# Attention loops issued in an order worked out from durations, with exponentials over three and two PSUM banks by turns, in place of fixed two-head steps

## Chip, cores, metric

One NeuronCore of a Trainium2 chip. The time is device microseconds (us) of one execution. The engines are PE (TensorE), ACT (ScalarE), DVE (VectorE), POOL (GpSimd) and SP (SyncE, which issues most DMAs). "PEld" is PE's weight load. The granted clock (PEclk) is the share of full speed that the profile shows PE was given.

## What is computed

Four layers in a row on x of 2048 x 512 (bf16), each `x = x + f(layernorm(x))`: spectral filter A, attention B, A, B again with the same weights.

```python
def _A_ref(x, w_r, w_i):                        # S = 2048, D = 512
    X = rfft2(x.astype(float32), axes=(-2, -1))
    return irfft2(X * (w_r + 1j * w_i), s=(S, D), axes=(-2, -1)).astype(bfloat16)

def _B_ref(x, wq, wk, wv, wo):                  # H = 32 heads of Dh = 16; k and v shared by all heads
    q = (x @ wq).reshape(B, S, H, Dh).transpose(0, 2, 1, 3)
    k, v = x @ wk, x @ wv
    p = softmax(einsum("bhqd,bkd->bhqk", q, k) * Dh ** -0.5, axis=-1)
    o = einsum("bhqk,bkd->bhqd", p, v)
    return o.transpose(0, 2, 1, 3).reshape(B, S, H * Dh) @ wo
```

## The kernel before

The Fourier transforms are matrix products. Attention is a loop over 32 series in each of the two B layers: a series is 512 queries x 4 heads. A *unit* is one block of 128 keys of one series and head: 128 x 512 scores, in one PSUM bank. There are 2048 units in a loop. A unit's exponentials are made in one of two ways:

- an *A unit* by ACT, with its exponential function, two units (two banks) in one instruction; one value product follows;
- a *D unit* by DVE, which turns scores into the bit pattern of a power of two (an int16 read as bf16). Four such tables, shifted against each other by 32 of 128 steps of an octave, are averaged through four value products. DVE makes the first table from PSUM; shifts of it come from DVE (128 x 2048 at a time) and POOL (128 x 1024).

Score products have 16 live of 32 contracted rows, so four fit beside each other into PE's rows; value products have 32 output columns, so four fit into PE's columns. I call four value products side by side a *quad*. A *turn* is a change of PE between products of different shape: score products, value products (and zero products like them, below), and products of the whole array such as projections.

The step of the loop is fixed by a plan: two A units of one ACT instruction, in most steps one D unit, and six value products. Twice in a usual series (`flags` false) there is no D unit; there a piece of a query or output projection is put in.

```python
    def plan(qb, s):                                     # key blocks for D units; which steps take one
        if (qb, s) == (NQB - 1, 7):
            return (1, 4, 7, 10), [a < 16 for a in range(24)]
        if (qb > 0 and s in (1, 2)) or (qb, s) == (0, 0):
            return (2, 5, 9, 12), [a % 3 != 2 for a in range(24)]
        return (1, 4, 7, 10, 13), [a % 11 != 10 for a in range(22)]

    def do_step(self, a_units, u, n):                    # [...] cut
        if u is not None:
            sd = self.ps.tile("b", [P, 512], F32)        # bank of the D unit
            self.scores(u, sd)
        if a_units:
            sa = self.ps.tile("sa", [P, 2, 512], F32)    # two banks, two buffers
            for m, au in enumerate(a_units):
                self.scores(au, sa[:, m, :])
            e = self.sb.tile("e", [P, 2, 512], BF)
            nc.scalar.activation(out=e, in_=sa, func=ACT.Exp, bias=EXP_LN, scale=SCALE)
        # [...] DVE's first table, shifts on DVE and POOL
        for z in pvs:                                    # of two steps ago, and D terms
            self.pv(*z)
        if u is None and self.first_pieces and self.step > 4:
            self.first_pieces.pop(0)()                   # transposes, keys, values of the last tokens
        elif u is None and self.pieces and self.step - self.last_piece > 4:
            self.last_piece = self.step
            self.pieces.pop(0)()                         # a whole projection: 4 or 5 products

    def qproj(self, qb, g, use_scalar):
        pq = self.ps.tile("b", [P, 512], F32)
        for cc in range(NC):                             # NC = 4
            nc.tensor.matmul(pq, lhsT=c.wq[:, cc, g * P:(g + 1) * P], rhs=xTq[:, cc, cols], ...)
```

PSUM's eight banks: scores "two" 2 x 2 banks, "one" 2 (accumulators of the loop; transposes of the spectral stage), "b" 2 (D scores, projections). The two spectral stages that matter here are `stage1` (transposes and a first product, one for each quarter `t` of the tokens) and `stage2`. All four query projections of the first queries stand ahead of the loop.

The softmax here doesn't subtract the row's maximum and nothing guards it: scores larger than these inputs give would overflow.

## Time and profile before

Median of five runs 1621.35 us (1615.95 to 1624.67). In the profile, 1620.2 us:

| stretch | us | ACT busy | PE busy |
|---|---|---|---|
| first loop, first exponential to end of the last | 679.2 | 98% | 99% |
| from there to the second loop | 113.5 | 34% | 86% |
| second loop | 680.7 | 98% | 99% |

The table of busy times by stretch, kernel before (start:end, length, then busy us and instructions of each engine, granted PE clock, DMA share, GB/s):

```profile
core 0: us, PE busy (x) PEld busy (x) DVE busy (x) ACT busy (x) POOL busy (x), PEclk, DMA share, GB/s
...
124.40:803.60 679.20, 672.16 (x6051) 192.34 (x6048) 631.18 (x1077) 666.08 (x723) 325.20 (x315) 0.99 0.05 16
803.60:917.10 113.50, 97.23 (x613) 51.51 (x612) 80.67 (x172) 38.47 (x53) 8.21 (x17) 0.95 0.01 3
917.10:1597.80 680.70, 671.48 (x6049) 191.93 (x6046) 618.27 (x1039) 666.33 (x723) 324.78 (x315) 0.99 0.06 18
```

PE and ACT are both full in the loops, so busy time does not say which of them sets the pace. The chain of waits (the work that ended last, followed back), by engine, names PE:

```profile
PE 79%; DVE 13%; DMA 3%; issue 3%; POOL 1%; ACT 1%; SPq 0%; DVEq 0%; POOLq 0%; ACTq 0%
```

The groups of the loop (busy us, mean ns of one | idle before, and what ended it):

```profile
L541 ACT ACTIVATE e<-sa 128x1024 bf16<-128x1024 f32 x1440 | 1329.4, 1142 | 24.2 <-PE sa L434 22.8
L516 POOL TENSOR_SCALAR t<-t 128x1024 int16<-128x1024 int16 x608 | 636.8, 1048 | 691.9 <-DVE t L511 513.8
L544 DVE TENSOR_SCALAR t<-b 128x512 int16<-128x512 f32 x1216 | 790.9, 681 | 61.6 <-PE b L434 56.1
...
L434 PE MATMUL sa<-QT,KT 32*128 32x512 bf16 x2880 | 563.7, 383 | 2.1 <-ACT e L541 2.1
```

ACT's exponential shows 1142 ns as a mean, but that is from start to end of instructions that overlap: 1440 of them are busy for 1329 us, 0.923 each. The timeline of ACT shows the rhythm (start, length of a run of instructions without idle time, count, idle time before it):

```profile
299.73 24.93 ACT L541 ACTIVATE e<-sa 128x1024 bf16<-128x1024 f32 x27
325.01 5.61 ACT L541 ACTIVATE e<-sa 128x1024 bf16<-128x1024 f32 x6 [0.36 <-PE sa L434]
330.98 5.61 ACT L541 ACTIVATE e<-sa 128x1024 bf16<-128x1024 f32 x6 [0.36 <-PE sa L434]
```

Read one instruction at a time, the ends of two exponentials lie 0.917 us apart wherever they follow without idle time. I call what a step takes beyond that a *gap*, and measure it from end to end. The gaps add up to 18.9 us in the first loop and 20.4 in the second (the prediction has 19.1 and 20.6; how small a gap is still counted makes the difference). About 6.4 us of each are in the first 25 us. Most others are 0.46 us, and the timeline of PE shows what stands there (here the gap at 324.7):

```profile
322.88 0.39 PE L434 MATMUL sa<-QT,KT 32*128 32x512 bf16 x2
323.20 0.39 PE L447 MATMUL acc<-e,V 128*32 128x512 bf16 x2
323.52 1.04 PE L494 MATMUL b<-wo_sb,ON 128*128 128x512 bf16 x4
324.49 0.39 PE L434 MATMUL b<-QT,KT 32*128 32x512 bf16 x1
324.49 0.39 PE L434 MATMUL sa<-QT,KT 32*128 32x512 bf16 x2
```

The next scores follow the last ones after 1.61 us, as a whole output projection (four products, 0.97 us to the next scores) lies between them.

### The profile page before, as it was taken

What the parts mean: (1) busy time and instruction counts of PE and PEld (TensorE: products, weight loads), DVE (VectorE), ACT (ScalarE), POOL (GpSimd) and SP (SyncE); (2) the same over time, 40 slices, a digit from 0 to 9 for tenths busy, and PEclk for the clock granted to TensorE, in tenths of its full rate; (3) what the DMA queues carried; (4) which work ended last, traced back from release to release, by engine and by line L of the source; (5) the groups of instructions that cost most, each with busy time, mean ns of one, the idle gap of its engine ahead of it and who ended that gap; (6) DMA issues with size and microseconds to landing.
All of it is one profiled execution on the core that took longest, in us unless ns stands there. A gap on an engine that the chain in (4) does not pass through costs nothing.

```text
span 1620.2 us, 34219 instructions
## 1 busy us (share of the span) xinstructions
PE 1541.9 (95%) x13320; PEld 488.3 (30%) x13320; DVE 1421.4 (88%) x2476; ACT 1425.7 (88%) x1570; POOL 682.3 (42%) x696
## 2 busy tenths in 40 slices
PE   4899999999999999999988999999999999999996
PEld 2542222222222222222344322222222222222221
DVE  6777999989998999899958789998899889998994
ACT  6248999999999999999823699999999999999994
POOL 3013545445553455445400145454445444544542
PEclk9998999999999999999999899999999999999998
DMA  6000000000000000000000000000000000000000
GB/s 190 0 1 1 17 16 17 17 16 17 17 17 10 17 17 17 17 17 17 17 7 1 1 8 17 17 17 27 19 13 18 21 23 16 17 20 25 18 16 29
DMA packets 44916, 31.75 MB, mean 20 GB/s; under 512 B 25553, under 2 KB 35793, under 8 KB 44625
## 3 DMA queue, kind: packets, MB, share of 16 engines
q1 hardware_dynamic: 44368, 28.51, 5.9%
q8 instruction: 104, 1.70, 0.4%
q0 software_dynamic: 384, 1.05, 0.2%
q14 instruction: 60, 0.48, 0.1%
HBM read 24.43 MB, written 2.62 MB: 17 GB/s over the span
## 4 chain that ended last, share of the span: by engine, by line
PE 79%; DVE 13%; DMA 3%; issue 3%; POOL 1%; ACT 1%; SPq 0%; DVEq 0%; POOLq 0%; ACTq 0%
PE acc L447 37%; PE b L434 21%; PE sa L434 9%; DVE t L544 4%; DVE t L511 3%; PE b L391 2%; PE one L328 2%; DMA rb<-rd 2%; PE two L266 2%; PE b L494 2%; PE two L242 1%; DVE odd L479 1%; DVE ON L476 1%; PE two L270 1%; PE two L268 1%
## 5 line engine op out<-in xcount | busy, mean ns | idle before, releaser
L541 ACT ACTIVATE e<-sa 128x1024 bf16<-128x1024 f32 x1440 | 1329.4, 1142 | 24.2 <-PE sa L434 22.8
L516 POOL TENSOR_SCALAR t<-t 128x1024 int16<-128x1024 int16 x608 | 636.8, 1048 | 691.9 <-DVE t L511 513.8
L544 DVE TENSOR_SCALAR t<-b 128x512 int16<-128x512 f32 x1216 | 790.9, 681 | 61.6 <-PE b L434 56.1
L447 PE MATMUL acc<-t,V 128*32 128x512 bf16 x4864 | 732.8, 385 | 0.0
L447 PE MATMUL acc<-e,V 128*32 128x512 bf16 x2880 | 569.2, 392 | 0.0
L434 PE MATMUL sa<-QT,KT 32*128 32x512 bf16 x2880 | 563.7, 383 | 2.1 <-ACT e L541 2.1
L434 PE MATMUL b<-QT,KT 32*128 32x512 bf16 x1216 | 467.3, 385 | 14.0 <-DVE t L544 11.9
L511 DVE TENSOR_SCALAR t<-t 128x2048 int16<-128x2048 int16 x608 | 417.3, 687 | 0.0
L434 PEld LDWEIGHTS <-KT 32*128 32x128 bf16 x4096 | 204.8, 90 | 619.9 <-issue 612.9
L447 PEld LDWEIGHTS <-V 128*32 128x32 bf16 x7744 | 159.8, 93 | 330.2 <-issue 330.2
L176 POOL TENSOR_TENSOR rstd<-mv,eps 128x4 f32<-128x4 f32 x16 | 3.3, 209 | 186.0 <-DVE mv L169 186.0
L168 DVE BATCH_NORM_STATS2 stats<-x_sb 128x6 f32<-128x512 bf16 x64 | 43.4, 687 | 15.5 <-ACT x_sb L330 8.5
L273 ACT CAST Xs<-two 128x1024 bf16<-128x1024 f32 x16 | 16.2, 1012 | 40.7 <-PE two L270 40.7
L266 PE MATMUL two<-Y,TAB 128*128 128x512 bf16 x128 | 48.5, 379 | 0.1
L456 DVE COPY den<-acc 128x512 f32<-128x512 f32 x64 | 43.6, 682 | 1.0 <-PE acc L447 1.0
L495 DVE TENSOR_TENSOR x_sb<-b,x_sb 128x512 bf16<-128x512 f32 x32 | 21.9, 690 | 23.5 <-PE b L494 23.3
L315 PE MATMUL two<-TAB,V 128*128 128x512 bf16 x128 | 33.8, 396 | 7.8 <-DVE V L288 7.8
L330 ACT CAST x_sb<-one 128x512 bf16<-128x512 f32 x32 | 18.5, 586 | 21.4 <-PE one L328 21.1
L242 PE MATMUL two<-tab_PH,xTA 128*128 128x512 bf16 x128 | 33.2, 414 | 4.0 <-DVE xTA L236 3.0
L270 PE MATMUL two<-Y,TAB 128*128 128x256 bf16 x128 | 34.9, 273 | 0.0
L268 PE MATMUL two<-Y,TAB 128*128 128x256 bf16 x128 | 34.9, 272 | 0.0
L494 PE MATMUL b<-wo_sb,ON 128*128 128x512 bf16 x120 | 33.4, 394 | 0.4 <-DVE x_sb L495 0.4
(82 smaller groups left out, 609.0 us busy)
## 6 DMA issues: line engine op xcount, KB each, us to landing
rb<-rd SPq DMA_DIRECT2D x64, 256.0 KB
x_sb<-in_A_x_dram SPq DMA_DIRECT2D x4, 512.0 KB
ON<-odd SPq DMA_DIRECT2D x120, 16.0 KB
TAB<-const_TAB SPq DMA_DIRECT2D x1, 1024.0 KB
wr_sb<-in_A_w_r_dram SPq DMA_DIRECT2D x4, 256.0 KB
wi_sb<-in_A_w_i_dram SPq DMA_DIRECT2D x4, 256.0 KB
dq<-den SPq DMA_DIRECT2D x64, 8.0 KB
rd<-dq SPq DMA_DIRECT2D x64, 8.0 KB
```

Source lines behind the costliest of these rows:

```text
L242: nc.tensor.matmul(pm[:, q, :], lhsT=xT[:, pair, q, cc, :], rhs=c.PH[:, cc, :], start=(cc == 0), stop=(cc == NC - 1))
L266: nc.tensor.matmul(pm, lhsT=TAB[:, t, j2, (COS + n) % 4, :], rhs=yt, start=(t == 0), stop=False, skip_group_check=True)
L268: nc.tensor.matmul(pm[:, LO], lhsT=TAB[:, t, j2, (SIN + n + 2) % 4, :], rhs=yt[:, HI], start=False, stop=False, skip_group_check=True)
L270: nc.tensor.matmul(pm[:, HI], lhsT=TAB[:, t, j2, (SIN + n) % 4, :], rhs=yt[:, LO], start=False, stop=(t == T - 1), skip_group_check=True)
L434: self.nc.tensor.matmul(out, lhsT=self.c.KT[32 * i:32 * i + 32, half, kc * P:(kc + 1) * P], rhs=self.A.QT[32 * i:32 * i + 32, g, qb * 512: ...
L447: self.nc.tensor.matmul(self.acc[key][32 * i:32 * i + 32, :], lhsT=self.c.V4[:, kc, j, :], rhs=e, start=first, stop=False, skip_group_chec ...
L456: nc.vector.tensor_copy(out=den, in_=self.acc.pop(key))
L494: nc.tensor.matmul(po, lhsT=o[:, r * P:(r + 1) * P], rhs=w, start=(k == 0), stop=(k == len(parts) - 1))
L511: nc.vector.tensor_scalar(out=tj, in0=cyc["t0"], scalar1=float(SH[j]), scalar2=None, op0=ALU.add)
L516: nc.gpsimd.tensor_scalar(out=cyc["t1"][:, h, :], in0=tj[:, h, :], scalar1=1.0, scalar2=float(SH[1] - SH[j]), op0=ALU.mult, op1=ALU.add)
L541: nc.scalar.activation(out=e, in_=sa, func=ACT.Exp, bias=EXP_LN, scale=SCALE)
L544: nc.vector.tensor_scalar(out=self.dcyc[c]["t0"][:, k, :], in0=sd, scalar1=Y_MUL, scalar2=Y_ADD, op0=ALU.mult, op1=ALU.add)
```

## The change

Intent: let ACT pay its fixed part less often (three banks, then two, in one instruction), pack value products into full quads, and issue on all engines in an order that a small model of their durations finds, so that none waits. The core of the diff (the model, some 500 lines, is cut; the lines shown are a selection, some shortened, with comments added):

```diff
     ps = Arena(ctx.enter_context(tc.tile_pool(name="ps", bufs=1, space=bass.MemoryType.PSUM)),
-               {"two": 2, "one": 2, "b": 2}, {"acc": "one", "sa": "two"})
+               {"a3": 1, "a2": 1, "acc": 1, "b": 2}, {})
@@ stage1 of the spectral filter
-            pt = ps_.tile("one", [P, 2, NC, P], BF)
+            pt = ps_.tile("b", [P, 2, NC, P], BF)
@@ ahead of the loop
-                for g in range(4):
-                    at.qproj(0, g, g % 2 == 0)
+                at.qproj(0, 0, nc.scalar.copy)
@@ after the first loop: the filter's memory is lent to the loop and loaded again
+            load_filter(nc.gpsimd, c, sb, A_w_r, A_w_i)
@@ the loop
+QUAD, ACT_FIX, ACT_UNIT = 0.225, 0.05, 0.4267
+PSUM_OP, WIDE_OP, POOL_OP = 0.6, 0.6, 1.05
+    def scores(self, with_a):                      # three A units, then two, and up to two D units
+            n, units, self.a_next = self.a_size, self.a_next, []
+            self.a_size = 5 - n
+            sa = self.ps.tile(f"a{n}", [P, n, 512], F32)
+    def quad(self, t, full):                       # one value product for each of the four heads
+    def filler(self):                              # zero weights: adds nothing to the accumulator
+        for i in range(4):
+            self.nc.tensor.matmul(out[32 * i:32 * i + 32, :], lhsT=self.c.zw, rhs=self.c.wo[:, 0, :], ...)
+    def pool(self):                                # POOL's shift waits for DVE's wide shift two back
+            if h >= 2:
+                ready = max(ready, self.halves[h - 2].get("s_end", NEVER) + 0.16)
+    def ask_queries(self):                         # a projection is two tasks of two products
+            m1 = self.add("PE", 2 * QUAD, first, at=at, bank=True)
+            m2 = self.add("PE", 2 * QUAD, lambda ...: self.A.qproj_mm(qb, g, tile["pq"], (2, 3)), [m1])
+    def run(self):                                 # the engine whose model time is least goes next
+        while self.v_cur < self.n_series:
+            turns[min(self.t, key=self.t.get)]()
```

In numbers of instructions: 582 exponentials of 1536 elements and 583 of 1024 in place of 1440 of 1024; 2912 A units and 1184 D units in place of 2880 and 1216; products with zero weights, which I call fillers.

## The prediction

> **What bounds the kernel now.** The two attention loops take 679 and 681 us of 1620 (124.4-803.6 and 917.1-1597.8 in the table of busy times by stretch). There ACT is busy 98%, PE 99%, DVE 91-93%, POOL 48%. The chain of waits gives PE 79%, but where a loop runs smoothly the 128x1024 exponentials end exactly 0.917 us apart (675 of 719 steps of the first loop in the timeline), each starting before the last has ended: ACT sets the pace, 1440 x 0.917 = 1320 us. The rest, 19.1 and 20.6 us, is where two ends lie further apart: 6.4 us at each loop's start (last tokens' transposes, keys, values), and twenty steps of 1.38 us where a projection sits on PE between score groups.
>
> **What the change does.** It replaces fixed steps (2 heads for ACT, mostly 1 for DVE, 6 value products) by an order worked out from durations.
>
> - ACT: exponentials of 1536 and 1024 alternate, 582 + 583 for 1440. Casts of 512 and 1024 take 0.586 and 1.012 us, so 512 elements cost 0.427; the fixed part of a pipelined exponential is 0.917-0.853 = 0.064. A 1536 then takes 1.343; the sum is 1316 us, only 4 less, as ACT now takes 2912 units, not 2880 (DVE 1184, not 1216).
> - PE: value products go in fours into the four column groups, in longer batches: 1290 turns between score and value products a loop, not 1440. The Trainium skill, "TensorEngine Tiling", section "Tiling Modes", says a mode switch drains TensorE; the trace agrees in size: two value products take 0.32 us in the chain, six 0.54, so a turn costs about 0.1. I count 951 value slots, 583 score slots, 250 filler slots, 150 projections of 0.215 us and the turns: 550 us of 660. PE gets slack despite 1940 fillers.
> - DVE: operations issue every 0.60 us; 592 conversions, 296 shifts and 80 us more: 610 us a loop, 92%, as before.
> - PSUM: scores hold 3 + 2 banks, one buffer each; the accumulator falls to one, so a series' end holds value products up for one evacuation (0.68 us).
> - Three first query projections move into each loop: 12 products of 0.22 us, 2.6 us each time.
> - Filters are loaded again through POOL; landed before use.
>
> **Critical path.** The gain is mostly the 40 us of ACT gaps, not the wider exponential. I expect about 15 us to return as small stalls: single score buffers leave PE 0.917 us to refill the wide one.
>
> 1621 - 4 (ACT work) - 40 (gaps) + 15 (new stalls) - 5 (projections) = 1587 us; range 1571 to 1612. Faster by over 2%: 0.53; within 2%: 0.43; slower: 0.04.
>
> **What would show it.** Loops of 664-670 us; ACT 98-99% busy there; narrow exponentials ending 0.92 us after a wide one, wide ones 1.34; no 6 us at the loop's start; stretches outside the loops a few us shorter, their groups unchanged.
>
> **What would make it wrong.** PE, in its fixed order, waits for DVE's bank or the single accumulator and ACT starves: idle above 30 us a loop. DVE and POOL collide: the skill's "SBUF — State Buffer", section "Who interferes with whom", says DVE's fast modes and GpSimd lock each other out (no run shows it yet). Shifts longer than 0.69 or 1.05 us would show it. A granted clock below 0.99 in the loops. A longer tail after the last exponential.

## The result

Median 1593.40 us (1591.18 to 1597.06, 8 runs) against 1622.04 (15 runs). The ratio is 0.9831, 95% interval 0.9816 to 0.9845. Ratios are the mean time of one kernel's fast runs over that of the other's of the same rounds, so not quite the ratio of the medians quoted. That is faster, by less than 2%.

The same stretches of the changed kernel, first loop, between the loops, second loop:

```profile
120.70:790.30 669.60, 640.36 (x7031) 197.54 (x7027) 624.94 (x1051) 663.26 (x586) 332.39 (x313) 0.99 0.07 19
790.30:908.50 118.20, 96.80 (x615) 51.01 (x605) 79.80 (x167) 38.08 (x52) 8.61 (x17) 0.94 0.01 3
908.50:1571.00 662.50, 632.68 (x6970) 196.88 (x6967) 616.94 (x1023) 658.77 (x583) 326.23 (x309) 0.99 0.06 19
```

The loops are 9.6 and 18.2 us shorter, ACT is busy over 99% in them, PE 96%; the stretch between the loops is 4.7 us *longer*. The chain of waits, by engine and by line, has turned over:

```profile
ACT 51%; PE 24%; issue 12%; DVE 8%; DMA 4%; POOL 1%; SPq 0%; POOLq 0%; DVEq 0%; ACTq 0%
ACT e L827 50%; PE acc L673 7%; PE a L614 5%; DMA rb<-rd 2%; PE a L282 2%; PE b L614 2%; PE acc L798 1%; DVE tB L851 1%; DVE spare L875 1%; PE acc L348 1%; DMA rd<-dq 1%; PE a L258 1%; DVE stats L177 1%; PE a L284 1%; PE a L286 1%
```

Half the span is now a chain of exponentials alone, where before the pieces of PE's steps made it up. The groups, with the two shapes of the exponential apart, and the fillers:

```profile
L827 ACT ACTIVATE e<-a 128x1536 bf16<-128x1536 f32 x582 | 967.6, 1663 | 9.1 <-PE a L614 4.5 <-PE b L614 4.4
L827 ACT ACTIVATE e<-a 128x1024 bf16<-128x1024 f32 x583 | 723.2, 1241 | 1.5 <-PE acc L673 1.2
...
L614 PE MATMUL a<-QT,KT 32*128 32x512 bf16 x2912 | 460.6, 383 | 48.5 <-ACT e L827 35.9 <-ACT x_sb L350 1.3
...
L899 POOL TENSOR_SCALAR tA<-tA 128x1024 int16<-128x1024 int16 x298 | 320.5, 1078 | 341.4 <-DVE tB L851 263.8 <-PE b L614 38.3 <-PE acc L673 26.3
...
L798 PE MATMUL acc<-wo_sb,zw 128*32 128x512 bf16 x1868 | 184.0, 388 | 0.0
```

The timeline of ACT in the first loop (a run is named after its first shape; wide and narrow alternate):

```profile
199.22 38.85 ACT L827 ACTIVATE e<-a 128x1536 bf16<-128x1536 f32 x34
238.52 67.90 ACT L827 ACTIVATE e<-a 128x1536 bf16<-128x1536 f32 x60 [0.46 <-PE a L614]
306.75 11.40 ACT L827 ACTIVATE e<-a 128x1536 bf16<-128x1536 f32 x10 [0.32 <-PE b L614]
```

The window cuts the first run: it began at 138.5 us and has 88 exponentials. Runs of 88 and 60 without a break, and later one of 294, have taken the place of runs of 6 to 121, mostly with 0.36 us between them. Ends lie 1.343 us apart at a wide one and 0.917 at a narrow one, so the exponentials alone are 582 x 1.343 + 583 x 0.917 = 1316 us, 4 less than 1440 x 0.917 = 1320. The gaps are 9.6 and 6.1 us, 15.6 in place of 39.2 (sums of unrounded values).

Where the 28.5 us between the two profiles come from:

| stretch | before, us | after, us | difference |
|---|---|---|---|
| start to first product of stage 2 | 43.3 | 42.9 | -0.4 |
| stage 2 to first exponential, first loop | 81.1 | 77.8 | -3.3 |
| first loop | 679.2 | 669.6 | -9.6 |
| last exponential to stage 2 | 33.5 | 40.0 | +6.5 |
| stage 2 to first exponential, second loop | 80.0 | 78.2 | -1.8 |
| second loop | 680.7 | 662.5 | -18.2 |
| last exponential to the end | 22.4 | 20.7 | -1.7 |

The one loss is behind the first loop. PE's timeline there, kernel before (803.65 is the end of the last exponential):

```profile
803.86 0.39 PE L447 MATMUL acc<-e,V 128*32 128x512 bf16 x2
...
804.84 0.61 PE L232 MATMUL one<-tab_ident,ec 128*128 128x128 bf16 x8
...
806.75 3.63 PE L242 MATMUL two<-tab_PH,xTA 128*128 128x512 bf16 x16 [0.60 <-DVE xTA L236]
...
815.34 0.60 PE L494 MATMUL b<-woz_sb,odd 128*128 128x512 bf16 x2 [1.82 <-DVE odd L479]
```

The last queries' output projection needs `odd`, and for `odd` the softmax's divisors go through DRAM and back, which takes some 10 us. Before, PE does the next layer's transposes (L232) in that time. The changed kernel:

```profile
790.39 0.39 PE L673 MATMUL acc<-e,V 128*32 128x512 bf16 x2
...
792.45 0.38 PE L344 MATMUL acc<-x_sb,tab_ident 128*128 128x512 bf16 x1
800.92 1.03 PE L740 MATMUL b<-woz_sb,odd 128*128 128x512 bf16 x2 [8.09 <-DVE odd L704]
...
805.97 0.61 PE L248 MATMUL b<-tab_ident,ec 128*128 128x128 bf16 x8
```

PE stands still for 8.1 us and begins the transposes (L248) at 806.0, 15.6 us after its last value product. Two half-done projections hold both "b" banks, and the transposes now need one of those.

### The profile page after: what moved, and what is told of

The parts are those of the page before. It is cut to its first block, busy times and chain, and to the rows that moved or that the text cites. A ratio compares the mean times of both kernels' runs of the same rounds, so it can differ in the third digit from the quotient of the medians.

```text
span 1591.7 us, 36765 instructions
## 1 busy us (share of the span) xinstructions
PE 1468.0 (92%) x15204; PEld 497.1 (31%) x15204; DVE 1412.5 (89%) x2430; ACT 1414.4 (89%) x1293; POOL 691.0 (43%) x689
## 3 DMA queue, kind: packets, MB, share of 16 engines
q0 software_dynamic: 1024, 3.15, 0.7%
## 4 chain that ended last, share of the span: by engine, by line
ACT 51%; PE 24%; issue 12%; DVE 8%; DMA 4%; POOL 1%; SPq 0%; POOLq 0%; DVEq 0%; ACTq 0%
ACT e L827 50%; PE acc L673 7%; PE a L614 5%; DMA rb<-rd 2%; PE a L282 2%; PE b L614 2%; PE acc L798 1%; DVE tB L851 1%; DVE spare L875 1%; PE acc L348 1%; DMA rd<-dq 1%; PE a L258 1%; DVE stats L177 1%; PE a L284 1%; PE a L286 1%
## 5 line engine op out<-in xcount | busy, mean ns | idle before, releaser
L827 ACT ACTIVATE e<-a 128x1536 bf16<-128x1536 f32 (+1 forms) x1165 | 1319.1, 1452 | 10.6 <-PE a L614 4.5
L614 PE MATMUL a<-QT,KT 32*128 32x512 bf16 x2912 | 460.6, 383 | 48.5 <-ACT e L827 35.9
L899 POOL TENSOR_SCALAR tA<-tA 128x1024 int16<-128x1024 int16 x298 | 320.5, 1078 | 341.4 <-DVE tB L851 263.8
L899 POOL TENSOR_SCALAR spare<-spare 128x1024 int16<-128x1024 int16 x294 | 318.1, 1085 | 317.6 <-DVE tB L851 253.5
L673 PE MATMUL acc<-tB,V 128*32 128x512 bf16 x2368 | 428.5, 386 | 0.1
L875 DVE TENSOR_SCALAR spare<-b 128x512 int16<-128x512 f32 x588 | 387.4, 684 | 32.5 <-PE b L614 28.9
L875 DVE TENSOR_SCALAR tA<-b 128x512 int16<-128x512 f32 x596 | 391.8, 682 | 26.6 <-PE b L614 21.7
L673 PE MATMUL acc<-tA,V 128*32 128x512 bf16 x1192 | 257.5, 389 | 1.6 <-DVE den L691 1.4
L673 PE MATMUL acc<-spare,V 128*32 128x512 bf16 x1176 | 247.7, 387 | 3.9 <-DVE den L691 2.8
L851 DVE TENSOR_SCALAR tB<-tA 128x2048 int16<-128x2048 int16 x298 | 208.0, 704 | 3.3 <-PE acc L673 2.3
```

What stands on the lines that cost most here:

```text
L614: self.nc.tensor.matmul(out, lhsT=self.c.KT[32 * i:32 * i + 32, half, kc * P:(kc + 1) * P], rhs=self.A.QT[32 * i:32 * i + 32, g, qb * 512: ...
L673: self.nc.tensor.matmul(self.acc[32 * i:32 * i + 32, :], lhsT=self.c.V4[:, u[1], j or 0, :], rhs=e, start=(u[0], i) not in self.seen, stop ...
L827: self.nc.scalar.activation(out=e[:, 0:k, :], in_=sa[:, 0:k, :], func=ACT.Exp, bias=EXP_LN, scale=SCALE)
L851: inst = nc.vector.tensor_scalar(out=tb, in0=half["tA"], scalar1=float(SH[1]), scalar2=None, op0=ALU.add)
L875: nc.vector.tensor_scalar(out=half["tA"][:, 0, m, :], in0=sd, scalar1=Y_MUL, scalar2=Y_ADD, op0=ALU.mult, op1=ALU.add)
L899: inst = self.nc.gpsimd.tensor_scalar(out=half["tA"][:, 1, :, :], in0=half["tA"][:, 0, :, :], scalar1=1.0, scalar2=float(SH[2]), op0=ALU.m ...
```

## Experiments

Twelve kernels ran. Medians of the kernel before in their rounds were 1619.4 (e1, e2, e3, e5), 1620.1 (e4, e6, e7, e8), 1623.1 (e9, e10, e11) and 1620.8 (e12). "Loops" and "gaps" are read from the profiled run, both loops added. The rounds ran on three chips (0, 4 and 9 in the record), so runs of different rounds are best compared by their ratios. The diffs below are cut to the telling lines.

| run | median us | ratio to before, 95% | loops us | gaps us |
|---|---|---|---|---|
| before | 1622.0 | 1 | 1359.9 | 39.2 |
| changed | 1593.4 | 0.983 (0.982-0.985) | 1332.1 | 15.6 |
| e1 no fillers | 1646.7 | 1.017 (1.013-1.021) | 1385.0 | 74.0 |
| e2 pairs | 1626.4 | 1.005 (1.003-1.008) | 1362.6 | 34.6 |
| e3 pairs, two accumulators | 1618.8 | 1.001 (0.999-1.003) | 1356.6 | 32.3 |
| e4 queries first | 1602.4 | 0.989 (0.987-0.990) | 1331.9 | 17.3 |
| e5 transposes in accumulator's bank | 1592.1 | 0.984 (0.982-0.986) | 1332.2 | 15.7 |
| e6 before, half projections | 1603.5 | 0.990 (0.988-0.991) | 1343.9 | 23.2 |
| e7 no order of shifts | 1634.4 | 1.010 (1.008-1.011) | 1369.4 | 55.9 |
| e8 as e5, second stage only | 1590.0 | 0.981 (0.980-0.983) | 1331.1 | 14.6 |
| e9 before, fillers at the start | 1619.0 | 0.997 (0.996-0.999) | 1353.7 | 33.0 |
| e10 e8 with ACT's measured fixed part | 1600.5 | 0.986 (0.985-0.988) | 1342.5 | 27.8 |
| e11 pairs, other first key blocks | 1634.0 | 1.007 (1.005-1.008) | 1372.1 | 45.9 |
| e12 e8 with fillers twice | 1629.2 | 1.005 (1.003-1.007) | 1372.1 | 55.6 |

All gave correct results but e6, which is wrong on purpose.

The theory at this point: ACT's exponentials set the pace of the loops, and the change won by closing the gaps between them. Rivals: the width of the exponential carries the gain; the fillers carry it by keeping PE's clock up; the gaps are not of PE's making.

### e1_no_fill: the changed kernel without fillers

```diff
     def filler(self):
+        return False
```

> The changed kernel without any filler product on PE (1980 of them gone; the order, worked out anew, gives ACT 2900 units and DVE 1196). Theory (ACT's exponentials set the pace of the loops, 580 pairs of 1.343 + 0.917 = 1311 us, and what the change won is mostly the gaps between them): within 6 us of the changed kernel's 1593, so 1585 to 1599, granted clock in the loops 0.98 or more. Rival (the fillers keep PE's granted clock up and so earn their place): the clock in the loops falls below 0.95 and the time rises by over 15 us.

Measured: 1646.7 us, 53 more than the changed kernel, and the mean granted clock 0.916. My theory missed, the rival holds. Stretches of this run: the two loops, then 3.4 us ahead of one drop of the clock, then the drop itself:

```profile
121.90:815.70 693.80, 623.99 (x6007) 178.13 (x6027) 631.42 (x1063) 663.78 (x583) 334.74 (x317) 0.91 0.06 18
932.00:1623.20 691.20, 618.83 (x6017) 179.63 (x6038) 623.66 (x1029) 663.22 (x581) 333.36 (x311) 0.92 0.06 18
165.20:168.60 3.40, 1.66 (x22) 0.50 (x20) 2.94 (x5) 3.29 (x3) 1.48 (x2) 1.00 0.00 0
168.60:182.30 13.70, 13.44 (x93) 2.64 (x93) 11.55 (x20) 10.25 (x9) 4.95 (x5) 0.50 0.04 9
```

In the 3.4 us ahead of the drop PE was busy for 1.66; then the clock is 0.50 for 13.7 us, PE fills up at half speed, and ACT, at 10.25 of 13.7 us, starves. Inside the two loops the clock was halved for 242 us in all, in the changed kernel for 24, and 64 of this run's 74 us of gaps overlap such stretches. The Trainium skill, "TensorE: Matmul & The Clock Gate", section "What's actually happening", describes this: the clock is gated down to half unless PE is active, decided in windows of about 3.4 us. The trace agrees: the clock is 1.00 or 0.50, and low stretches in the loops last 3.4 us or a multiple of it, up to 17.1.

### e2_pairs: the worked-out order with exponentials of two banks only

```diff
-        while len(self.a_next) < self.a_size:
+        while len(self.a_next) < 2:
@@
-            sa = self.ps.tile(f"a{n}", [P, n, 512], F32)
+            sa = self.ps.tile(f"a{n}", [P, n, 512], F32)[:, 0:2, :]
```

> The changed kernel with two heads in every exponential (1448 of 128x1024, none of 1536), all else left, the order worked out anew. Theory: the wide exponential is worth only its saved fixed parts, 1448 x 0.917 = 1328 us against 1316, so about 12 us slower than the changed kernel: 1605, range 1599 to 1613, with the gaps between exponentials still under 10 us a loop. Rival (the width is where the gain comes from): the time returns to 1617 or more.

Measured: 1626.4 us, 33 slower than the changed kernel, and 0.5% slower than the kernel before. Of the 30.5 us in its loops, 11.6 are the exponentials (1448 x 0.917 = 1328), as expected; 19 are gaps, which were to stay small and did not. Turns are 1442 and 1439, against 1291 and 1284, and PE is busy 96% with fewer fillers. So this order without the wide exponential does not win anything: by the time, the rival holds (but see e10 on what an order alone can do).

### e3_pairs_acc2: pairs, and the free bank as a second accumulator

```diff
-               {"a3": 1, "a2": 1, "acc": 1, "b": 2}, {})
+               {"a3": 1, "a2": 1, "acc": 2, "b": 2}, {})        # "a3" has two banks here
```

> As the run with pairs alone, but the PSUM bank that is set free becomes a second accumulator, as the kernel before had it. 1444 x 0.917 = 1324 us of exponentials. Theory (one accumulator costs little, as only value products wait for its evacuation): within 4 us of the run with pairs after the 4 us of its smaller ACT share, so 1597 to 1607. Rival (the single accumulator is a real price of the wide scores): 8 us or more below the run with pairs.

Measured: 1618.8, 7.7 below e2 by the medians, 6.7 by the profiles. In the loops it is 6.0: 3.7 are four exponentials fewer (1444), 2.3 gaps. A second accumulator is worth little; the size is at the edge of what I had allowed. The absolute range was missed, as e2 had missed it.

### e4_q_first: all four first query projections ahead of each loop

```diff
-                at.qproj(0, 0, nc.scalar.copy)
+                for g in range(4):
+                    at.qproj(0, g, nc.scalar.copy if g % 2 == 0 else nc.vector.tensor_copy)
```

> The changed kernel with all four first query projections ahead of each loop, as the kernel before had them. Theory (PE is the limit there, 12 products of 0.22 us): the stretch from stage 2 to the first exponential, 77.8 and 78.2 us in the changed kernel, grows by 2 to 3 us each time, to about 80.5, as in the kernel before (81.1 and 80.0); the loops change by under 2 us; about 1597 in all. Rival (the shorter stretch comes from the new PSUM layout): both stretches stay at 78.

Measured: the stretches from stage 2 to the first exponential are 80.5 and 81.0 us (changed: 77.8 and 78.2; before: 81.1 and 80.0), and the loops 1331.9 in place of 1332.1. So the moved products are worth 2 to 3 us in each layer: in the ten kernels with one projection ahead of the loop these stretches are 77.7 to 79.8 us, in the four with all of them (before, e4, e6, e9) 80.0 to 81.6. A cost inside the loop does not show, but the order there was worked out anew, so a small one is not excluded. The timed median is 9 us above the changed kernel's, the profile, which is of the fastest of its executions, 5.5; the rest is not explained.

### e5_acc_transpose and e8_acc_second: transposes in the accumulator's bank

```diff
-            pt = ps_.tile("b", [P, 2, NC, P], BF)
+            pt = ps_.tile("acc", [P, 2, NC, P], BF)      # e8: "b" in the first spectral layer, "acc" in the second
```

> The changed kernel with the transposes of the spectral stage in the accumulator's bank, not in the two banks that the half-done output projections of the last queries hold. Theory (from the end of the first loop to stage 2 the changed kernel takes 40.0 us, before 33.5, as the transposes wait for those banks): that stretch returns to 33 to 35 us and the time is 6 us below the changed kernel: 1587, range 1583 to 1590; the loops unchanged. Rival (the stretch is longer because the scheduler puts the projections first, whatever the bank): no change, 1593.

> The changed kernel with the transposes in the accumulator's bank only after the first loop; ahead of the first loop they keep the two banks of the changed kernel, as the single bank cost 3.8 us there. Theory: 42.9 us to stage 2 as in the changed kernel, 36.0 us from the last exponential of the first loop to stage 2 as in the run with the bank moved everywhere, so about 4 us less than the changed kernel, 1589, range 1585 to 1592. Rival (the two moves hang together through the whole program's order): no gain.

Measured: in e5 the stretch behind the first loop falls from 40.0 to 36.0 us, but the start to stage 2 grows from 42.9 to 46.7, as one bank holds up the transposes there; together nothing (1592.1). In e8 only the second is moved: 43.3 and 35.9 us, 1590.0, and 4.1 us less than the changed kernel by the profiles. The intervals of the two ratios overlap, so the gain rests on that stretch. PE's timeline of e8 there:

```profile
790.21 0.39 PE L674 MATMUL acc<-e,V 128*32 128x512 bf16 x2
...
792.27 0.61 PE L249 MATMUL acc<-tab_ident,ec 128*128 128x128 bf16 x8
...
794.11 3.62 PE L259 MATMUL a<-tab_PH,xTA 128*128 128x512 bf16 x16
...
801.00 0.38 PE L741 MATMUL b<-woz_sb,odd 128*128 128x512 bf16 x1 [1.23 <-DVE odd L705]
```

The transposes start 2 us after the last value products, and PE works until `odd` is there. That the banks held them up is shown: this stretch is 38.6 to 40.2 us in the seven kernels with the transposes in "b" (changed, e1 to e4, e7, e11) and 34.8 to 36.3 in the four with the accumulator's bank (e5, e8, e10, e12). The banks explain about 4 of the 6.5 us. The other 2.5 are no more than the stretch varies by itself: in e9, whose code there is that of the kernel before, it takes 36.4 us in place of 33.5. The clock is halved for 10.2 us of it in e9, e8 and the changed kernel, and for 6.9 in the kernel before. e8 is the fastest version.

### e6_before_half_work: the kernel before with half the products of each projection

```diff
-        for cc in range(NC):
+        few = NC // 2 if qb else NC
+        for cc in range(few):
@@ project
+        else:
+            parts = parts[2:]
```

> The kernel BEFORE with half the products of every projection inside its loops (two instead of four for each query piece, about half for each output piece); wrong results on purpose. Theory (the 0.46 us gaps between exponentials are steps in which a projection of four products, 0.86 us, stands on PE between two score groups, and the two score buffers hide only some 0.2 us of it): with two products the lag is 0.64 + 0.1 + 0.43 - 0.917 = 0.25 us and is hidden; the gaps past the first 25 us of each loop, 12.6 and 13.9 us in all, fall to under 4 us, and the time falls by about 20 us to 1600. Rival (the gaps come from DVE, which must empty the projection's bank, or from the bank itself): the gaps keep two thirds of their size and the time falls by under 8 us.

Measured: 1603.5 us. Past the first 25 us of each loop the gaps fall from 12.6 and 13.9 us to 5.1 and 5.3. The size is a little under the theory's, but far from the rival's. What stood between two score groups on PE made most of those gaps. That splitting these pieces in two, as the changed kernel does, closes them as well was not tested alone: this run leaves products out, which also takes work from PE.

### e7_no_order: POOL's and DVE's shifts not kept apart

```diff
-            start = max(half["pool"] + LAT, self.pool_end)
+            start = half["pool"] + LAT
-            if h >= 2:
-                ready = max(ready, self.halves[h - 2].get("s_end", NEVER) + 0.16)
@@
-                    self.tc.add_manual_dep(inst.ins, self.s_inst[h - 2].ins.name, ...)
```

> The changed kernel without the rule that keeps DVE's wide shift and POOL's shift apart (no added wait of POOL for the shift two back, no regard of POOL's end in the order). Theory of the lock (DVE in its fast mode and POOL shut each other out): shifts of the two engines now overlap in time of issue and grow, DVE's wide shift from 0.70 us to over 0.8 or POOL's from 1.08 to over 1.2 on average, and the loops grow by 5 us or more. Rival (the rule does nothing on the chip): means within 0.03 us of the changed kernel's and time within 3 us of 1593.

Measured: 1634.4 us, 41 more. The groups of POOL's shift and DVE's wide shift, first in e7, then DVE's in the changed kernel, whose POOL group stands above (1078 ns):

```profile
L897 POOL TENSOR_SCALAR tA<-tA 128x1024 int16<-128x1024 int16 x300 | 387.9, 1293 | 277.8 <-DVE tA L875 258.7 <-DVE dq L696 11.2 <-PE a L614 7.3
...
L851 DVE TENSOR_SCALAR tB<-tA 128x2048 int16<-128x2048 int16 x300 | 235.3, 789 | 1.6 <-PE acc L673 1.4
```

```profile
L851 DVE TENSOR_SCALAR tB<-tA 128x2048 int16<-128x2048 int16 x298 | 208.0, 704 | 3.3 <-PE acc L673 2.3 <-POOL tA L899 0.9
```

POOL's mean goes from 1078 to 1293 ns and DVE's from 704 to 789, with the same shapes. Within e7 the 496 POOL shifts of this line and of `spare` that overlap a wide shift of DVE take 1337 ns on average, the 100 others 1050. The commonest overlapping pairs (440) take 1.58 us from the first start to the last end, the pairs of the changed kernel that only touch 1.64: side by side they win next to nothing (spans on POOL are rough). The order is worked out anew here too, so the 41 us are not all sure to be this. The Trainium skill, "SBUF — State Buffer", section "Who interferes with whom", states that DVE in its 2-port modes and GpSimd exclude each other for a whole instruction, through a shared pair of ports. The trace agrees as far as it goes, with longer instructions when the two are let loose; it does not show the port. The prediction named this risk, and missed that the change contains the cure.

### e9_before_fill_start: the kernel before with 12 filler quads at the start of each loop

```diff
+        if 1 <= self.step < 10:
+            self.fill(4 if self.step == 1 else 1)       # zero products into the first accumulator
```

> The kernel BEFORE with a few zero products (12 quads in steps 1 to 9 of each loop, added to the first accumulator). In the kernel before the granted clock is 0.5 for 13.7 us at the start of each loop, after a stretch in which PE waits about half the time. Theory (an under-used PE loses its clock, and that makes most of the 6.4 us gap at the loop's start): the half-clock stretch shrinks to 7 us or vanishes, each loop is 2 to 4 us shorter, 1616 in all against 1621. Rival (the gap is the waiting of the last tokens' transposes, keys and values, whatever the clock): loops within 1 us of before, or longer by the added products' time.

Measured: 1619.0 against 1623.1 in the same rounds; the loops 2.4 and 3.9 us shorter. The start of the first loop, kernel before:

```profile
124.20:127.60 3.40, 2.34 (x18) 0.65 (x11) 2.73 (x6) 3.40 (x5) 1.20 (x2) 1.00 0.03 5
127.60:141.30 13.70, 13.46 (x69) 3.94 (x67) 6.73 (x13) 10.39 (x12) 2.12 (x3) 0.50 0.00 0
```

and e9:

```profile
124.80:128.20 3.40, 3.31 (x42) 1.11 (x42) 2.66 (x7) 3.40 (x5) 1.24 (x2) 1.00 0.02 5
128.20:141.80 13.60, 12.61 (x132) 4.55 (x132) 9.87 (x18) 12.91 (x15) 3.23 (x4) 1.00 0.01 2
```

PE was busy for 2.34 of 3.4 us (its longest idle time there is 1.06 us), and that cost 13.7 us at half clock. Filled, the clock stays. The gaps of the first 25 us fall from 6.3 and 6.4 us to 2.6 in each loop. More than half of what I had put down to the last tokens' transposes was the clock.

### e10_fit: e8 with ACT's fixed part as measured

```diff
-ACT_FIX, ACT_UNIT = 0.05, 0.4267
+ACT_FIX, ACT_UNIT = 0.064, 0.4267
```

> The changed kernel with the transposes of the second spectral stage in the accumulator's bank and with the order worked out for the measured fixed part of an exponential, 0.064 us in place of 0.05. ACT takes 2908 units (1315 us). Theory (the exponentials set the pace, what is left are 15 us of gaps, some from an order that runs ahead of the chip): loops 1 to 3 us shorter in sum than the 1331 of the run without it, so about 1588, range 1583 to 1592. Rival (the order's durations no longer matter at this size; gaps are chance of where the clock drops): within 2 us of 1590 either way, with gaps at other places.

Measured: 1600.5, ratio 0.986; gaps 20.7 and 7.1 us. Neither theory had this: a constant nearer to the truth made the first loop 10 us longer. The trace shows where: the clock was halved for 27.3 us of that loop (13.7 in e8), and 12.2 us of its gaps overlap these stretches (4.2 in e8). One of them, from the timeline, and in the last line the 3.4 us ahead of the drop, in which PE was busy for 1.74:

```profile
472.59 0.69 DVE L705 TENSOR_TENSOR odd<-den,rb 128x512 bf16<-128x512 f32 x1 [1.92 <-DMA rb<-rd]
...
474.54 0.37 PE L615 MATMUL b<-QT,KT 32*128 32x512 bf16 x1 [1.65 <-DVE spare L876]
...
475.18 1.45 ACT L828 ACTIVATE e<-a 128x1536 bf16<-128x1536 f32 x1 [1.23 <-PE a L615]
...
472.70:476.10 3.40, 1.74 (x19) 0.41 (x15) 3.40 (x6) 2.17 (x3) 1.31 (x2) 1.00 0.06 15
```

DVE waits for the divisors from DRAM (`rb`), PE, in its fixed order, for a bank that DVE has to empty, and ACT for PE's scores; then the clock is at half for 6.8 us. So a small wait can cost twice. Why this order has more of them than e8's is not shown; the order is worked out anew from any change, and here that made 10 us. All differences between runs with different orders have to be read with that in mind: e2, e3 and e11 against the changed kernel above all.

### e11_pairs_start: pairs, with other first key blocks

```diff
-        self.avail[0] = [0, 1, 2, 3, 4, 5, 6, 7, 12, 13, 14, 15, 8, 9, 10, 11]
+        self.avail[0] = [0, 1, 2, 3, 4, 5, 6, 7, 8, 9, 12, 13, 14, 15, 10, 11]
```

> As the run with pairs alone, but ACT takes key blocks 8 and 9 ahead of the last tokens' blocks, so that it doesn't run dry at 141 us (one gap of 4.7 us in each loop there). Theory: that gap goes and nothing else changes: about 9 us faster than the run with pairs, 1617, which leaves some 24 us for the width: 11 of exponentials and the rest of gaps, as 1440 turns a loop leave PE less room than 1290. Rival (the gap is not of the pairs' order but of the transposes themselves): the gap moves and the time stays at 1626.

Measured: 1634.0. The gap of 4.7 us at 141 us is gone, as it should be, but gaps of 4.7 and 6.2 us stand at 516 and 666 us of the first loop. The test of the width is not cleaner for it: pairs gave 32 to 46 us of gaps in three orders, three and two banks by turns 16 to 28 in three (changed, e4, e10; e5 and e8 have the changed kernel's). How much of the gaps belongs to the width stays open; the 8 to 12 us of ACT's fixed parts are sure. Nor was the packing into full quads, with its fewer turns, tested alone.

### e12_double_fill: e8 with every filler written twice

```diff
-        for i in range(4):
+        for i in (0, 1, 2, 3) * 2:
```

> As the run with the accumulator's bank after the first loop only (1590), with every filler product written twice: 3960 in place of 1980, and nothing else in any engine's order changed. Theory (the gaps that are left in the loops, 14.6 us, sit mostly at short drops of PE's clock, at 234.7, 627.3 and 1019.8 us in that run): the drops inside the loops past the first 25 us vanish, the gaps fall by 2 to 5 us, 1587 in all, range 1583 to 1590. Rival (the second copy, 0.22 us each, stands in the way of score groups, as PE has no more room than the fillers fill): the gaps grow and the time rises by 5 us or more.

Measured: 1629.2, 39 us more, with no other instruction moved. The two loops:

```profile
122.40:813.10 690.70, 677.34 (x8028) 204.91 (x8028) 627.70 (x1051) 671.42 (x586) 331.54 (x313) 0.99 0.07 19
928.00:1609.40 681.40, 666.10 (x7906) 201.92 (x7904) 619.94 (x1023) 665.08 (x583) 325.97 (x309) 0.99 0.06 18
```

PE is busy 98% and ACT 97 and 98%, and the drops of the clock are still there (240.7, 687.9 and 1046.3 us). The rival holds: fillers only pay in time that is truly free. None costs 53 us, twice as many 39; the model puts them where they fit.

## Why the prediction was right, point by point

The forecast was 1587 us, range 1571 to 1612; 1593.4 was measured. The mechanism in the sum held, with one term missing. Its odds leaned the other way: 0.53 for a gain of over 2%, where 1.7% was measured.

| term | predicted, us | measured, us |
|---|---|---|
| ACT's exponentials | -4 | -4.3 (1320.5 to 1316.2) |
| gaps closed, less new stalls | -40 + 15 | -23.6 (39.2 to 15.6) |
| projections moved into the loops | -5 | -5.1 in the profile; 4 to 5.5 by e4 |
| stretch behind the first loop | not in the sum | +6.5, of which about 4 by the banks (e5, e8) |
| start and end | 0 | -2.1 |

- *"I expect about 15 us to return as small stalls."* 15.6 us of gaps are left, but that is in part luck. 8.6 of them stand in the first 25 us of the loops, where the prediction wanted the old gap gone; only 7.0 come later, 5.5 of these at wide exponentials, as it had expected.
- *ACT sets the pace.* Right: ends of 1.343 and 0.917 us, ACT over 99% busy, loops of 669.6 and 662.5 us. PE's 79% in the chain of waits did not mean that PE set the pace: most of the later gaps came from PE's steps (e6), but 675 of 719 steps of the first loop kept ACT's 0.917 us.
- *"The gain is mostly the 40 us of ACT gaps, not the wider exponential."* Right as a sum of the stretches, wrong as a statement of causes. With two banks in every exponential the same scheduler gives 1626 or 1634, and 1619 with a second accumulator (e2, e11, e3). Part of the gaps closes only with the width, or by an order that the width allows; how much is open (e10).
- *"PE gets slack despite 1940 fillers."* The slack was right and the word "despite" wrong. Slack on PE is what the fillers are there to hide: without them the clock is halved for 242 us of the loops (e1).
- *"No 6 us at the loop's start."* Half right: 4.2 and 4.4 us are left of 6.3 and 6.4.
- *"Stretches outside the loops a few us shorter."* Ahead of the loops yes; behind the first one 6.5 us longer. The prediction named a longer tail as a risk and did not look at which banks the transposes had been given, though the diff shows it.
- *DVE and POOL collide.* They do if let (e7, +41 us); the change orders them.

## What to carry to other kernels

When two engines look full, look at the ends of the longest repeated instruction: if they keep one distance, that engine sets the pace, and what is to be won is the sum of the places where they do not. Work that is taken off PE can cost more than it saves once PE's clock falls; zero products in truly idle time hold it, and more of them than fit cost nearly as much as none (39 us against 53 here). When PSUM banks change hands for one stage, check who else needs them in the stages around it, and test an order that a program works out in several variants before a small difference is explained.

## What the Trainium skill lacked or had wrong

- "TensorE: Matmul & The Clock Gate", section "Why this matters for your kernels", advises "No PE-idle gaps >~3µs between matmul bursts". That alone does not keep the clock: in the kernel before it fell to 0.50 for 13.7 us after 3.4 us in which PE was busy for 2.34 and its longest idle time was 1.06 us; in e1 after 1.66 of 3.4 busy, with no idle time over 1.6 us. (The page itself says elsewhere, in "A second HAM failure mode: psum-queue depth-cycling", that frequent short idle times make the clock swing.)
- No page states how busy PE must be. In the loops of 14 profiles the clock falls 81 times, always whole multiples of 3.41 us apart within a profile. In the 3.41 us ahead of a fall PE was busy 46 to 83%, with no idle time over 1.65 us. Cut by the same grid, no stretch under 60% kept the clock and none over 84% lost it; of those from 60 to 72%, 31 lost it and 22 kept it, so the busy share alone does not settle it in between.
- "TensorE: Matmul & The Clock Gate" does not give filling with zero products as a means, or its price: 0, 1980 and 3960 of them gave 1646.7, 1593.4 (1590.0 as e8) and 1629.2 us.
- "TensorEngine Tiling", section "Tiling Modes", says that a change of mode drains TensorE but gives no cost. In the kernel before, two value products between scores take 0.32 us of the chain and six take 0.54, so two quads cost 0.22 more than one, and a turn about 0.1 (an estimate: what is left of 0.32). As the page has no size, the prediction's "agrees in size" can mean only that the trace shows a cost.
- "SBUF — State Buffer", section "Who interferes with whom", gives the lock for single instructions. What it costs a loop that is full is in none of the pages I read: up to 41 us of 1593 here, as POOL's mean went from 1.08 to 1.29 us and DVE's from 0.70 to 0.79 (e7).
